# Mamba-2 scan and SiLU block on one core: last outputs transposed by TensorE, a piece of work moved behind unit 1's y, and paced weight loads

## The chip, the cores and the metric

The kernel runs on one core of a Trainium2 chip. The metric is the device time of one execution in microseconds (us). The kernel before the change takes 355.02 us, the median of 7 runs (354.64 to 357.64).

## The reference, cut to what matters

A Mamba-2 scan in chunks gives y for 4 batches, 8 heads, 768 positions and 32 values per head. The heads are laid side by side, which makes 3072 tokens of 256 values. A two-layer block with SiLU follows:

```python
M = CB * L                                   # C.B within a chunk, times decays
y[:, :, sl] = einsum(M, xc) + einsum(Cc, state) * exp(cum)
state = decay_full * state + sum(Bx)
x = y.transpose(0, 2, 1, 3).reshape(3072, 256)
h = x @ w_in                                 # 256 -> 2048
out = (h * (1 / (1 + exp(-h)))) @ w_out      # 2048 -> 256
```

The weights come in 64 bits per value and are turned into 32-bit floats on the chip.

## The kernel before, in words

**Units.** The tokens are cut into 12 units of 256. For each unit the scan makes y, and ScalarE copies it into the tile XM (`f_X`, L469). The first layer of a unit is 8 slots, `f_s1(g, j)` (L479). A slot is 8 matmuls of 128x256 and one SiLU, which writes two of the 16 blocks of the unit's gT. The second layer is a generator for a pair of units (`s2_pair`, L554), and `f_s2(n)` (L621) puts its next n matmuls into the program. From unit 4 on the layers use a scheme with seven instead of eight block products (`f_x1`; `segs` at L558 has the seven products of the second layer, named 1, w, 5, 7, 6, 4, 3).

**Order.** The order is written out by hand, and every engine works in program order. Lines 778 to 847 are the beginning. Unit 0's slots 0, 1 and 2 stand between the steps of unit 1's scan. Then come unit 1's y (`f_Y(1)`, L827), its copy (`f_X(1)`, L828), and the list `steps` (L833), whose entries are unit, slot and work for other engines: `b5` is `w_bits(5)`, `s6` is `w_size(6)`, and `E`, `D`, `T`, `C`, `G`, `Y` are steps of unit 2's scan. The loop at L855 holds unit 2's slots with the second layer of units 0 and 1, and unit 3's y in its last turn.

**Weights.** There are 16 pieces of 512 KB in 64 bits: 0 to 7 are w_in, 8 to 15 are w_out. `load_w(n)` (L150) has SP, the sync engine's queue, load one into one of 7 raw buffers. `w_size(n)` (L160) is two ScalarE instructions, L164 and L166. `w_bits(n)` (L168) is three VectorE instructions, L174, L176 and L178, and an addition on GpSimd, L182. It also posts the load of piece n + 7. Slot j of a unit needs piece j of w_in.

**Loads at the start.** SP posts pieces 0 to 2, then unit 1's B, C and x, then pieces 3 to 6 one after another (L206). Behind them in the same queue come pieces 7 and 8 and the loads of unit 2.

**Outputs.** Products have the model's 256 columns on the partitions and the tokens along them. `f_out` (L542) transposes a tile of 128x256 on VectorE, in blocks of 32x32 (L547), and posts four stores of 32 KB (L549), in which every run is 32 values, 128 bytes. The tile ot of the transposed values has two buffers. For the very last product, "3" of units 10 and 11, the work is split in halves of 128 tokens (L586 to L590). Each half has an addition on VectorE that reads the matmuls' result, a transposition on VectorE, and four stores of 16 KB, of which two go by SP and two by the queue of ScalarE:

```python
for k in range(2):
    nc.vector.tensor_tensor(out=pn[:, :, k], in0=on[:, :, k], in1=..., op=ALU.add)
    f_out(P, 0, 1, p["3"], (nc.sync, nc.scalar), (128 * k, 128 * k + 128))
```

Stores and loads by SP and ScalarE share eight completion semaphores in turn. A DMA instruction first waits until the DMA that last had its semaphore has landed.

Of the kernel before, what the change touches and what calls it, by code (L numbers as in the profile page):

```python
# [8 lines left out]
FP32 = mybir.dt.float32  # L9
# [12 lines left out]
def kernel(  # L22
# [56 lines left out]
    def at(u):  # L79
        return u // UPB, u % UPB * UT  # L80
# [37 lines left out]
    def load_x(u, q):  # L118
        b, t0 = at(u)
        xt[u] = loads.tile([128, 2, H, D], FP32, name="xt")  # L120
        for k in range(2):
            q.dma_start(out=xt[u][:, k], in_=x[b, :, t0 + 128 * k:t0 + 128 * k + 128].rearrange("h p d -> p h d"))
# [27 lines left out]
    def load_w(n, q):  # L150
        src, dst = w_piece(n)
        if src.dtype == FP32:
            q.dma_start(out=dst, in_=src)
            return
        t = raw[n] = rawp.tile([128, 2, WF, 2], U32, name="raw")
        q.dma_start(out=t.rearrange("p k f two -> p k (f two)"), in_=src.bitcast(U32))
# [11 lines left out]
    def w_bits(n, parts=1):  # L168
        dst = w_piece(n)[1]
        if n in raw:  # L170
            u, v, hi = wu.pop(n), wv.pop(n).bitcast(U32), raw[n][:, :, :, 1]


            nc.vector.tensor_scalar(out=u, in0=u, scalar1=LEAST, scalar2=MOST, op0=ALU.max, op1=ALU.min)  # L174
            u = u.bitcast(U32)
            nc.vector.tensor_scalar(out=u, in0=u, scalar1=3, scalar2=None, op0=ALU.logical_shift_left)  # L176

            nc.vector.scalar_tensor_tensor(out=v, in0=hi, scalar=0x80000000, in1=v,  # L178
                                           op0=ALU.bitwise_and, op1=ALU.bitwise_or)
            for i in range(parts):  # L180
                fs = slice(WF // parts * i, WF // parts * (i + 1))
                nc.gpsimd.tensor_tensor(out=dst[:, :, fs].bitcast(U32), in0=u[:, :, fs], in1=v[:, :, fs], op=ALU.add)  # L182
        if n + RAW < len(W):
            load_w(n + RAW, nc.sync)
# [18 lines left out]
    load_n(1, 0, nc.sync)  # L203
    load_n(1, 1, nc.sync)
    load_x(1, nc.sync)
    for n in range(3, RAW):  # L206
        load_w(n, nc.sync)


# [269 lines left out]
    def f_s1(g, j):  # L479
        if j == 0:  # L480
            GTS[g] = new_g()
        xm = XM[g].rearrange("p (w c) t -> p w (c t)", w=2)
        hp = ps_h.tile([128, 2, UT], FP32, name="hp")
        for i in range(2):
            f = 2 * j + i
            for kc in range(KC):
                nc.tensor.matmul(out=hp[:, i], lhsT=w_in_sb[:, kc, f * 128:(f + 1) * 128],  # L487
                                 rhs=xm[:, kc], start=(kc == 0), stop=(kc == KC - 1))
        nc.scalar.activation(GTS[g][:, :, j], hp, AF.Silu)  # L489
        if j == 7:  # L490
            XM.pop(g)
# [47 lines left out]
    def p_add(o, p, q, engine, op=ALU.add):  # L539
        engine.tensor_tensor(out=o, in0=p, in1=q, op=op)  # L540

    def f_out(P, i, v, c, queues=None, cols=None):  # L542

        b, t0 = at(2 * P + v)
        c0, c1 = cols or (0, UT)
        t = opool.tile([128, UT], FP32, name="ot")
        nc.vector.transpose(out=t[:, c0:c1], in_=c[:, c0:c1])  # L547
        for q in range(4):
            (queues or (nc.sync,))[q % len(queues or (0,))].dma_start(  # L549
                out=bass.AP(tensor=out.tensor, offset=out.offset + (b * S + t0 + c0) * d_model + 128 * i + 32 * q,  # L550
                            ap=[[d_model, 32], [32 * d_model, (c1 - c0) // 32], [1, 32]]),
                in_=t[32 * q:32 * q + 32, c0:c1].rearrange("p (b d) -> p b d", d=32))

    def s2_pair(P, final=False, joint=False):  # L554

        adder = nc.vector if final else nc.gpsimd
        p = {}
        segs = (("1", lambda j: wjo[:, 0, 0, j], lambda: gb(P, 0, 0)), ("w", lambda j: wjo[:, 1, 0, j], lambda: gb(P, 1, 0)),  # L558
                ("5", lambda j: SO[0][j // 4][:, j % 4], lambda: TN[P]),
                ("7", lambda j: SO[2][j // 4][:, j % 4], lambda: gb(P, 0, 1)),  # L560
                ("6", lambda j: SO[1][j // 4][:, j % 4], lambda: gb(P, 0, 0)),
                ("4", lambda j: wjo[:, 1, 1, j], lambda: gb(P, 1, 0)),
                ("3", lambda j: SO[3][j // 4][:, j % 4], lambda: gb(P, 1, 1)))

        def end(m, o):

            p[m] = ppool.tile([128, UT], FP32, name="ps")
            on = o.rearrange("p (c k t) -> p c k t", c=2, k=2)
            pn = p[m].rearrange("p (k c t) -> p c k t", c=2, k=2)
            if not (final and m == "3"):  # L570
                nc.scalar.activation(pn, on, AF.Copy)  # L571
            if m == "w":
                p_add(p["w"], p["w"], p["1"], adder)
                PEND.append(partial(f_out, P, 0, 0, p["w"]))
            elif m == "6":
                p_add(p["6"], p["6"], p["1"], adder)
                p_add(p["7"], p["7"], p["6"], adder)
                p_add(p["6"], p["5"], p["6"], adder, ALU.subtract)
                p_add(p["5"], p["5"], p["7"], adder, ALU.subtract)
                PEND.append(partial(f_out, P, 1, 1, p["5"]))  # L580
            elif m == "4":
                p_add(p["4"], p["4"], p["7"], adder)
                PEND.append(partial(f_out, P, 1, 0, p["4"]))
            elif m == "3" and final:

                for k in range(2):  # L586
                    nc.vector.tensor_tensor(out=pn[:, :, k], in0=on[:, :, k],
                                            in1=p["6"].rearrange("p (k c t) -> p c k t", c=2, k=2)[:, :, k],
                                            op=ALU.add)
                    f_out(P, 0, 1, p["3"], (nc.sync, nc.scalar), (128 * k, 128 * k + 128))  # L590
            elif m == "3":
                p_add(p["3"], p["3"], p["6"], adder)
                PEND.append(partial(f_out, P, 0, 1, p["3"]))

        last = NF // 2 - 1
        if joint:
            o = ps_o.tile([128, 2, UT], FP32, name="o_ps")
            for j in range(NF // 2):
                for n, (m, w, g) in enumerate(segs[:2]):
                    nc.tensor.matmul(out=o[:, n], lhsT=w(j), rhs=g()[:, j], start=(j == 0 and n == 0), stop=(j == last),  # L600
                                     skip_group_check=True)
                    if j == last and n == 1:
                        end("1", o[:, 0])
                        end("w", o[:, 1])
                    yield
        for n, (m, w, g) in enumerate(segs):
            if joint and n < 2:
                continue
            if final and n % 2 == 0:
                o = ps_h.tile([128, 2, UT], FP32, name="hp")[:, 0]  # L610
            else:
                o = ps_o.tile([128, 2, UT], FP32, name="o_ps")[:, 0]
            for j in range(NF // 2):
                nc.tensor.matmul(out=o, lhsT=w(j), rhs=g()[:, j], start=(j == 0), stop=(j == last))  # L614
                if j == last:
                    end(m, o)
                yield
# [3 lines left out]
    def f_s2(n):  # L621
        for _ in range(n):
            if S2 and next(S2[0], S2) is S2:
                S2.pop(0)
                f_s2(1)
# [197 lines left out]
    for k in range(2):  # L823
        f_M(1, k)
    f_s1(0, 2)
    w_bits(3)
    f_Y(1)  # L827
    f_X(1)  # L828
    w_size(4)
    w_size(5)  # L830
    w_bits(4)

    steps = ((1, 0, "b5 s6"), (1, 1, "b6 s7"), (0, 3, "b7 s8"), (1, 2, "b8"), (1, 3, "E D"), (0, 4, ""),  # L833
             (1, 4, ""), (0, 5, "T C s9"), (1, 5, "b9 s10"), (0, 6, "G"), (1, 6, "b10 s11"),
             (0, 7, "Y b11 s12"), (1, 7, "b12 s13"))

# [18 lines left out]
    for j in range(8):  # L855
        waiting, PEND[:] = PEND[:], []
        f_s1(2, j)
        if j == 7:
            scan_piece(3, 0, "Y")
        f_s2(2 if j < 2 else 4)  # L860
        if j < len(late):
            w_steps(late[j])
        if j == 2:
            scan_piece(3, 0, "T")
            for q in range(4):
                f_T1(0, q)
        if j == 3:
            f_SO(0)
        scan_piece(3, j, ("", "", "", "E", "DC", "", "G", ""))
        if j in (5, 6):  # L870
            f_SO((2, 1)[j - 5])
        outputs(waiting)
        if j in (2, 5):
            load_unit(4 + j // 3)

        for h in range(2):
            if j in (3, 5, 7):
                f_TS(0, {3: 3, 5: 2, 7: 4}[j], h)
# [88 lines left out]
```

## Time and profile before

| | |
|---|---|
| median of 7 runs | 355.02 us |
| the profiled execution | 354.92 us |
| its span (first to last instruction) | 353.2 us, so 1.72 us lie around it |
| TensorE matmuls (PE) | busy 342.0 us, 97% of the span |
| TensorE weight loads (PEld) | 287.0 us, 81% |
| VectorE (DVE) | 206.1 us, 58% |
| ScalarE (ACT) | 162.0 us, 46% |
| GpSimd (POOL) | 112.0 us, 32% |
| granted TensorE clock, mean | 0.999 |

Times in the timeline count from the start of the span. A row is start, duration, engine, line, operation, output <- input, shape and how often; brackets at its end hold the idle time before it and what ended it. An engine's name with a "q" is its instruction queue, in which DMAs are issued: the row's duration is that of the issue, not of the transfer. The table of waits gives engine, line, what was waited for, total us, times, and the longest.

### The profile page before, as it was taken

The numbers are of one execution on the slowest core, as the hardware profiler recorded it, in microseconds if no ns is written. First come the engines' busy times: TensorE is split into PE (matmuls) and PEld (weight loads), VectorE is DVE, ScalarE is ACT, GpSimd is POOL, SyncE is SP. The second block draws the span as 40 slices with busy tenths as digits, with TensorE's granted clock in tenths as the row PEclk, the third lists the DMA queues.
The fourth block names the chain that finished last, engine by engine and source line by source line (L and its number), as shares of the span: only waits on it lengthen the run. The fifth ranks groups of instructions, "written<-read, shape, count | busy, mean of one in ns | idle before, by whom it ended". The sixth has DMA issues, their size and how long they took to land.

```text
span 353.2 us, 8346 instructions
## 1 busy us (share of the span) xinstructions
PE 342.0 (97%) x3305; PEld 287.0 (81%) x3306; DVE 206.1 (58%) x409; ACT 162.0 (46%) x393; POOL 112.0 (32%) x137
## 2 busy tenths in 40 slices
PE   7979999999999999999999999999999999999993
PEld 3558888878888878888888888888888888888882
DVE  7979999966695754544663553664562322144722
ACT  2558675323313545354645454645445454453110
POOL 4434345353095041244041244041244112052100
PEclk9999999999999999999999999999999999999999
DMA  6998958899786799865189865166504337431203
GB/s 111 223 341 143 328 173 134 164 178 198 131 121 111 118 174 178 152 123 83 20 159 179 157 114 92 16 113 121 100 2 74 67 61 141 75 62 26 36 0 45
DMA packets 118236, 42.79 MB, mean 121 GB/s; under 512 B 103604, under 2 KB 110004, under 8 KB 118196
## 3 DMA queue, kind: packets, MB, share of 16 engines
q1 hardware_dynamic: 110756, 25.67, 36.3%
q0 software_dynamic: 4464, 16.25, 24.7%
q10 hardware_dynamic: 2976, 0.33, 0.7%
q8 instruction: 26, 0.43, 0.5%
q14 instruction: 14, 0.11, 0.1%
HBM read 22.83 MB, written 3.15 MB: 74 GB/s over the span
## 4 chain that ended last, share of the span: by engine, by line
PE 91%; DVE 4%; DMA 2%; issue 1%; ACT 0%; POOL 0%; SPq 0%; ACTq 0%; DVEq 0%
PE o_ps L614 35%; PE hp L669 28%; PE hp L487 15%; PE hp L614 3%; PE gy L463 3%; PE o_ps L600 2%; PE gy L454 2%; PE gy L400 2%; DVE E L299 1%; PE gy L385 1%; DVE wv L178 1%; DMA tbc<-in_C_dram 1%; DMA tbc<-in_B_dram 1%; DMA out_dram<-ot 0%; DVE gT L275 0%
## 5 line engine op out<-in xcount | busy, mean ns | idle before, releaser
L672 DVE TENSOR_TENSOR gT<-hp,p 128x256 f32<-128x256 f32 x64 | 26.9, 420 | 73.7 <-ACT p L683 37.8
L487 PE MATMUL hp<-XM,w_in_sb 128*128 128x256 f32 x256 | 59.7, 382 | 1.9 <-POOL w_in_sb L182 1.2
L614 PE MATMUL o_ps<-gT,w_out_sb 128*128 128x256 f32 x240 | 60.4, 379 | 0.0
L675 ACT ACTIVATE gT<-gT 128x256 f32<-128x256 f32 x96 | 39.7, 414 | 44.0 <-DVE gT L672 44.0
L487 PEld LDWEIGHTS hp<-XM,w_in_sb 128*128 128x128 f32 x256 | 47.9, 190 | 10.0 <-POOL w_in_sb L182 2.3
L540 POOL TENSOR_TENSOR ps<-ps 128x256 f32<-128x256 f32 x35 | 29.4, 839 | 73.8 <-ACT ps L571 72.5
L669 PE MATMUL hp<-raw 128*128 128x256 f32 x192 | 52.7, 380 | 0.0
L614 PEld LDWEIGHTS o_ps<-gT,w_out_sb 128*128 128x128 f32 x240 | 45.4, 190 | 6.3
L535 POOL DMA_DIRECT2D gT<-gT x31 | 27.1, 911 | 68.1 <-DVE TN L526 21.5
L669 PEld LDWEIGHTS hp<-raw 128*128 128x128 f32 x192 | 36.2, 190 | 5.4 <-POOL ps L540 0.6
L683 ACT ACTIVATE p<-hp 128x256 f32<-128x256 f32 x64 | 24.6, 384 | 27.4 <-PE hp L669 25.9
L672 DVE TENSOR_TENSOR gT<-hp,u 128x256 f32<-128x256 f32 x32 | 13.6, 424 | 39.3 <-PE hp L669 39.3
L669 PE MATMUL hp<-XM,w_in_sb 128*128 128x256 f32 x128 | 34.1, 389 | 0.0
L489 ACT ACTIVATE gT<-hp 128x512 f32<-128x512 f32 x32 | 19.0, 595 | 30.2 <-PE hp L487 30.2
L669 PEld LDWEIGHTS hp<-XM,w_in_sb 128*128 128x128 f32 x128 | 23.3, 190 | 4.3 <-issue 1.0
L299 DVE TENSOR_TENSOR_SCAN E<-ab,diag 128x256 f32<-128x256 f32 (+1 forms) x32 | 25.6, 841 | 0.4
L571 ACT ACTIVATE ps<-o_ps 128x256 f32<-128x256 f32 x38 | 14.5, 383 | 23.9 <-PE o_ps L614 21.0
L336 POOL TENSOR_TENSOR BT<-bn,E 128x256 f32<-128x256 f32 x12 | 9.6, 799 | 46.2 <-DVE E L299 40.9
L614 PE MATMUL o_ps<-gT,wv 128*128 128x256 f32 x88 | 22.2, 380 | 0.0
L614 PE MATMUL o_ps<-gT,wu 128*128 128x256 f32 x88 | 22.2, 380 | 0.0
L614 PE MATMUL o_ps<-gT,raw 128*128 128x256 f32 x80 | 20.6, 382 | 0.0
L669 PE MATMUL hp<-raw,w_in_sb 128*128 128x256 f32 x64 | 19.1, 380 | 0.0
(121 smaller groups left out, 518.2 us busy)
## 6 DMA issues: line engine op xcount, KB each, us to landing
gT<-gT POOLq DMA_DIRECT2D x31, 512.0 KB, 6.1
ab<-in_a_dram SPq DMA_DIRECT2D x40, 128.0 KB
raw<-in_moe_w_in_dram SPq DMA_DIRECT2D x8, 512.0 KB
raw<-in_moe_w_out_dram SPq DMA_DIRECT2D x8, 512.0 KB
xt<-in_x_dram SPq DMA_DIRECT2D x24, 128.0 KB
out_dram<-ot SPq DMA_DIRECT2D x92, 32.0 KB
bn<-in_B_dram SPq DMA_DIRECT2D x22, 64.0 KB
tbc<-in_C_dram SPq DMA_DIRECT2D x40, 32.0 KB
```

What stands on the lines that cost most here:

```text
L299: nc.vector.tensor_tensor_scan(out=E[u].rearrange("p k h t -> p (k h t)")[:, Q * g0:Q * (g0 + n)], data0=t.rearrange("p g t -> p (g t)"), ...
L463: nc.tensor.matmul(out=y[32 * q:32 * q + 32, 2 * w + c, 64 * k:64 * k + 64], lhsT=xc[64 * c:64 * c + 64, k, h], rhs=m[64 * c:64 * c + 64, ...
L487: nc.tensor.matmul(out=hp[:, i], lhsT=w_in_sb[:, kc, f * 128:(f + 1) * 128], rhs=xm[:, kc], start=(kc == 0), stop=(kc == KC - 1))
L489: nc.scalar.activation(GTS[g][:, :, j], hp, AF.Silu)
L535: nc.gpsimd.dma_start(out=o[:, js], in_=a[:, js], accum_op=ALU.add)
L540: engine.tensor_tensor(out=o, in0=p, in1=q, op=op)
L571: nc.scalar.activation(pn, on, AF.Copy)
L614: nc.tensor.matmul(out=o, lhsT=w(j), rhs=g()[:, j], start=(j == 0), stop=(j == last))
L669: nc.tensor.matmul(out=o, lhsT=w, rhs=x_, start=start, stop=True, skip_group_check=True)
L672: nc.vector.tensor_tensor(out=o, in0=p, in1=q, op=ALU.add)
L675: nc.scalar.activation(o, i, AF.Silu)
L683: nc.scalar.activation(o, i, AF.Copy)
```

## The change

1. **Paced loads.** Before pieces 5 and 6 are posted, SP posts a copy of 4 bytes out of piece 3's (then piece 4's) raw buffer into a new tile `mark`. It can be issued only when that piece has landed.
2. **Slot (0, 3)**, unit 0's fourth, moves from the third place of `steps` to just behind `f_Y(1)` and `f_X(1)`. `w_size(4)` and `w_bits(4)` move ahead of `f_Y(1)`; `E D` stays with the fifth entry of `steps`, and slot (0, 3) now stands ahead of the list.
3. **Second layer of units 0 and 1.** In the turns of the loop at L855 with four matmuls of it, these are asked for as two and two. In the last turn unit 3's y (`scan_piece(3, 0, "Y")`) now stands between them; before, it stood ahead of all four.
4. **The last product.** Each half is transposed by TensorE (a matmul against the identity into an hp buffer), copied to ot by ScalarE (first half) or VectorE (second half), and stored by one DMA of 64 KB whose runs are 512 bytes: the first half by SP, the second by ScalarE's queue.

```diff
+    mark = const.tile([1, RAW], U32, name="mark")
     for n in range(3, RAW):
+        if n > 4:
+            nc.sync.dma_start(out=mark[:, n:n + 1], in_=raw[n - 2][0:1, 0, 0, 0:1])
         load_w(n, nc.sync)
...
-                    f_out(P, 0, 1, p["3"], (nc.sync, nc.scalar), (128 * k, 128 * k + 128))
+                    tp = ps_h.tile([128, 512], FP32, name="hp")[:, 0:128]
+                    nc.tensor.transpose(out=tp, in_=p["3"][:, 128 * k:128 * k + 128], identity=ident)
+                    ot = opool.tile([128, UT], FP32, name="ot")[:, 0:128]
+                    if k == 0:
+                        nc.scalar.activation(ot, tp, AF.Copy)
+                    else:
+                        nc.vector.tensor_copy(out=ot, in_=tp)
+                    b, t0 = at(2 * P + 1)
+                    r = b * S + t0 + 128 * k
+                    (nc.sync, nc.scalar)[k].dma_start(out=out[r:r + 128, 0:128], in_=ot)
...
     f_s1(0, 2)
+    w_size(4)
     w_bits(3)
+    w_bits(4)
     f_Y(1)
     f_X(1)
-    w_size(4)
     w_size(5)
-    w_bits(4)
-
-    steps = ((1, 0, "b5 s6"), (1, 1, "b6 s7"), (0, 3, "b7 s8"), (1, 2, "b8"), (1, 3, "E D"), (0, 4, ""),
+    f_s1(0, 3)
+
+    steps = ((1, 0, "b5 s6"), (1, 1, "b6 s7"), (1, 2, "b7 s8"), (1, 3, "b8"), (0, 4, "E D"),
...
         f_s1(2, j)
+        f_s2(2)
         if j == 7:
             scan_piece(3, 0, "Y")
-        f_s2(2 if j < 2 else 4)
+        if j > 1:
+            f_s2(2)
```

`f_out` also loses its options for queues and columns, which nothing else used.

More of the change, by code (lines that the diff above doesn't have):

```diff
@@ L540, in p_add, with f_out @@
         engine.tensor_tensor(out=o, in0=p, in1=q, op=op)
-    def f_out(P, i, v, c, queues=None, cols=None):
+    def f_out(P, i, v, c):
         b, t0 = at(2 * P + v)
-        c0, c1 = cols or (0, UT)
         t = opool.tile([128, UT], FP32, name="ot")
-        nc.vector.transpose(out=t[:, c0:c1], in_=c[:, c0:c1])
+        nc.vector.transpose(out=t, in_=c)
         for q in range(4):
[L549 to L552, printed above, removed]
+            nc.sync.dma_start(
+                out=bass.AP(tensor=out.tensor, offset=out.offset + (b * S + t0) * d_model + 128 * i + 32 * q,
+                            ap=[[d_model, 32], [32 * d_model, UT // 32], [1, 32]]),
+                in_=t[32 * q:32 * q + 32].rearrange("p (b d) -> p b d", d=32))
     def s2_pair(P, final=False, joint=False):
```

## The prediction

> **What bounds the kernel now.** I read the page first, then the waits of PE, then the timeline of the three places where the waits or the end point. The page gives PE 97% of the span and the chain that ended last 91% PE, so only two things shorten it: time in which PE is idle, and time after its last matmul. The table of waits, asked for PE alone from 26 us to 348 us, has two lines:
>
> ```profile
> PE gy L454 <- ACT gT L489: 0.7, 1, 0.7
> PE hp L487 <- ACT XM L472: 0.7, 1, 0.7
> ```
>
> In these 322 us the table by stages gives PE 320.5 us busy, and the two lines are 1.4 us of the rest. Whatever other engines do there is covered. The first of the two in time is unit 1's copy of y:
>
> ```profile
> 24.51 1.24 PE L463 MATMUL gy<-E,xt 64*32 64x64 f32 x64
> 24.78 1.27 POOL L182 TENSOR_TENSOR w_in_sb<-wu,wv 128x512 uint32<-128x512 uint32 x1 [2.87 <-DVE wv L178]
> 25.79 0.60 ACT L472 ACTIVATE XM<-gy 128x512 f32<-128x512 f32 x1 [1.20 <-PE gy L463]
> 26.44 14.08 PE L487 MATMUL hp<-XM,w_in_sb 128*128 128x256 f32 x64 [0.69 <-ACT XM L472]
> ```
>
> PE ends unit 1's y at 25.75, ScalarE copies it until 26.39, and the next slot, (1, 0), can start at 26.44. Piece 3 of the weights (the POOL row) is ready at 26.05. The second is unit 3's y:
>
> ```profile
> 75.76 1.99 PE L487 MATMUL hp<-XM,w_in_sb 128*128 128x256 f32 x8
> ...
> 77.03 1.28 DVE L411 TENSOR_TENSOR E<-gy,E 128x512 f32<-128x512 f32 x2
> ...
> 78.45 0.58 PE L454 MATMUL gy<-cw,sm 32*64 32x64 f32 x24 [0.70 <-ACT gT L489]
> ```
>
> The bracket names ScalarE, but the row that ends just before is VectorE's L411, at 78.31; PE had ended its slot at 77.75. Third, the end, from the timeline, the chain and SP's waits. The last matmul ends at 347.62:
>
> ```profile
> 347.66 0.29 DVE L587 TENSOR_TENSOR ps<-hp,ps 128x128 f32<-128x128 f32 x1 [2.08 <-PE hp L614]
> 347.99 0.31 DVE L547 STREAM_TRANSPOSE ot<-ps 128x128 f32<-128x128 f32 x1
> 348.25 0.29 DVE L587 TENSOR_TENSOR ps<-hp,ps 128x128 f32<-128x128 f32 x1
> ...
> 348.73 0.31 DVE L547 STREAM_TRANSPOSE ot<-ps 128x128 f32<-128x128 f32 x1 [0.18 <-DMA out_dram<-ot]
> ```
> ```profile
> 350.64 0.32 SPq L549 DMA_DIRECT2D out_dram<-ot  x1
> ```
> ```profile
> 346.95 1.65 DMA out_dram<-ot
> ```
> ```profile
> SPq L549 <- DMA out_dram<-ot: 1.0, 1, 1.0
> ```
>
> All values of the second half are in SBUF at 349.04, yet the last store is issued at 350.64, because it waited 1.0 us for an earlier store (the last fence, from SP's waits). Eight stores by two queues are in the way, not the transposition. A store takes 1.65 us from issue to landing (the chain's row), so the last lands near 350.64 + 1.65 = 352.29, and the closing barrier takes 0.91 us to 353.2.
>
> **Slot (0, 3) behind unit 1's y.** After unit 1's y PE no longer needs the copy but piece 3, at 26.05; PE began 0.06 us after such a row at 21.90. That is 26.11. If VectorE works beside it (bits 4 now follows at once), the addition takes 1.39 as at 28.71 instead of 1.27, and PE starts at 26.23. Gain 26.44 - 26.11 = 0.33, or 0.21; I take 0.27. What hides the copy now is slot (0, 3), 1.73 us. On ScalarE `w_size(4)` stands ahead of the copy: from the end of a SiLU at 24.59 its two instructions (26.28 to 27.50, 1.22) last until 25.81, so the copy starts at 25.81 instead of 25.79; far from late, since PE wants it at 27.85. If piece 4 had not landed at 24.6, the copy would be late by as much (see the loads below). Slots 3 and on are one slot later in ScalarE's order, so `w_size(6)` starts near 30.2 instead of 29.05, but VectorE's work on pieces 4 and 5 is 1 to 2 us earlier; no slot comes to wait for its piece (slot (0, 5), which needs piece 5, runs at 38.5, piece 5 is converted at 32.5 even now).
>
> **Two matmuls ahead of unit 3's y.** Two matmuls of 0.43 us (8 take 1.73 in the chain) fill 77.75 to 78.61, and L411 has ended at 78.31. Their data are there: the accumulating DMA into gT was issued by POOL from 64.24 on, such DMAs land after 5.4 to 8.0 us, and the buffer o_ps was copied out at 75.24. So the whole 0.70 goes. What is late next: unit 3's slots need its copy. y ends near 79.98, the copy near 80.65, and PE has two matmuls, 0.86 plus about 0.2 of restart (1.92 instead of 1.73 in the row after y), until 81.0. A margin of 0.3; if it were gone, each 0.1 costs 0.1. Gain 0.70 to 0.40; I take 0.65.
>
> **Paced loads.** Two semaphore waits and two small DMAs more on SP. Behind them in SP's queue stand pieces 5 to 8, all loads of unit 2, and pieces 9 on. Between 18 us and 27 us the DMA moves 348 GB/s: 0.524 MB per piece is 1.51 us, and pieces 3 to 8 are just these 9 us. So piece 3 is complete near 19.5 and piece 4 near 21.0. Piece 5 is now posted near 20.9 (19.5 + landing + two issues of 0.45) where it was posted before 18.5; bytes of a store show up 0.8 us after its issue. So the line runs dry 0.5 to 0.8 us per mark, and all that follows comes 1 to 1.5 us later. Nothing before PE was waiting for a load in this stretch, so nothing is gained by it. Piece 5 (near 23.5) is read at 26.5; of unit 2, the decays are issued by 31.8 and read at 39.87; piece 9 is issued at 34.87 and read at 42.05, 7.2 us later, while a piece takes at most 6.0 us from its posting behind others (16.49) to ScalarE's reading it (22.49). Slack 1.2 us at the least there. Cost 0; bounds 0 and the rival below.
>
> **The last product.** Removed: two transpositions and eight stores. Added, per half: a weight load of 0.14 and a matmul of 0.27 (L351, same shape, 0.48 from the start of the load to the end), a copy from PSUM, one store. First half: addition ends 347.95, PE starts 0.11 later (as L454 after L411), ends 348.54; ScalarE starts 0.09 later; its copy lies between 0.28 (128 columns on the line through 0.384 for 256 and 0.595 for 512) and 0.39 (L434, 128x128); I take 0.30: 348.93, store issued, landed near 350.6. Second half: its addition follows at once, to 348.25; PE ends near 348.75; VectorE's copy is between 0.19 (L424, 64 columns) and 0.29 (L587); its buffer ot is free when product 4's stores have landed, 348.60, as before; done at 349.05. That is no earlier than the 349.04 of before. But its store is issued at 349.1 instead of 350.64, and it has no predecessor to wait for: 350.64 - 349.1 = 1.54 less. The one unknown is how long a store of 64 KB takes. No row shows one; 32 KB took 1.65. Below: as the last one of 16 KB, about 1.4 to SP's wait, gain 1.8. Above: the two halves one after the other, 1.65 each from 348.93, lands 352.2, gain 0.1. Loads show that bytes are cheap here (64 KB at 348 GB/s is 0.19 us), so I stay near the 32 KB row and add 0.2: gain 1.35.
>
> [...]
>
> **Sum.** 0.27 + 0.65 + 0 + 1.35 = 2.27. From the profiled execution, 354.92 - 2.27 = 352.65; it stands 0.1 below the median of 355.02. I predict 352.6. PE is gap-free between the places, so what is gained early is carried to the end: the triggers of all later transfers move with PE.
>
> **Rivals.**
> - *The store of 64 KB is slow, or the two halves queue.* For it: no row has this form, and both use the same engines. Against: the two copies are 0.1 apart and small. The end gains only 0.1 to 0.8, say 0.4: 354.92 - 0.92 - 0.4 = 353.6. Chance 0.17.
> - *A wait takes the place of the one removed:* piece 3 later than 26.4, or unit 3's copy after the two matmuls. For: margins of 0.3. Against: rows of two engines give the margin. Gains 0.2 instead of 0.92: 354.92 - 0.2 - 1.35 = 353.4. Chance 0.1.
> - *Slower: the marks hold SP's queue.* An SP issue behind a full queue took 3.3 to 3.5 us (tbc at 10.49 and 22.32). If both marks met this, everything behind comes 6.8 us later; with the least slack of 1.2 to some 4 us, ScalarE stalls at piece 9 (42 us), SiLUs wait behind it and PE loses 2.8 to 5.6, say 4.2: 354.92 - 2.27 + 4.2 = 356.8. It decides when the delay passes about 2.3 plus the slack, 3.5 to 6.3 us. Against: the marks come when the queue holds just one piece. Chance 0.05.
> - The edits do what they say; the order of instructions on each engine leaves no doubt.
>
> **How the numbers follow.** The forecast has 0.68, own range 352.0 to 353.1 (gains 0.21 + 0.4 + 1.1 at the least, 0.33 + 0.70 + 1.8 at the most). With the two lesser gains the range is 351.9 to 353.8; it leaves out the slower case and the ends. Faster or slower by over 0.5%, 1.78 us, about what a measurement of this kernel can tell, means below 353.24 or above 356.8. Forecast nearly whole, and a third of the lesser gains, lie below: faster 0.76; same 0.20; slower 0.04.
>
> **What would show it.** Right: PE's waits from 26 us on have no L454 line, and at L487 at most 0.4; unit 3's y (L454) directly behind two matmuls of L614's group; last store issued 1.4 to 1.6 us after the last matmul (now 3.0); the end 4.1 to 4.3 after it (now 5.6). Wrong: a wait of ScalarE for a raw piece, PE idle between 30 and 50 us, or a store that takes over 2 us.

## The result and the profile after

The changed kernel takes 353.4 us (median of 18 runs, 352.69 to 354.68) against 355.12 us for the kernel before (47 runs, 354.25 to 357.64). The ratio is 0.9947, 95% interval [0.9935, 0.9958]: faster by 0.53%, with 0.42% to 0.65% as its bounds, so about at the 0.5% that the prediction set as measurable (the two medians alone are 0.48% apart). The forecast was 352.6, its range 351.9 to 353.8. The forecast's own part of that range, 352.0 to 353.1, does not hold the result; the wider range, which takes in the rivals' lesser gains, does. The profiled execution took 353.18 us, with a span of 351.5 us.

In the changed kernel the lines of the code have moved: f_s1's matmuls are L491 (were L487), the two parts of y L458 and L467 (L454, L463), the mark is L210, the transpositions of the last product are L595, their copies L598 and L600, their stores L603.

The table of PE's waits of the changed kernel, from 26 us on (engine, line, what was waited for, total us, times, longest):

```profile
PE hp L491 <- POOL w_in_sb L182: 0.7, 1, 0.7
PE hp L595 <- DVE ps L590: 0.4, 1, 0.4
```

The line of unit 3's y is gone, and the wait for the copy XM is now one for piece 3 on GpSimd (POOL). The second line is the new transposition, behind the last matmul. The timeline of the changed kernel at the first place:

```profile
24.68 0.86 PE L467 MATMUL gy<-E,xt 64*32 64x64 f32 x64
24.94 1.28 POOL L182 TENSOR_TENSOR w_in_sb<-wu,wv 128x512 uint32<-128x512 uint32 x1 [2.87 <-DVE wv L178]
...
25.79 0.59 ACT L476 ACTIVATE XM<-gy 128x512 f32<-128x512 f32 x1
...
26.27 1.99 PE L491 MATMUL hp<-XM,w_in_sb 128*128 128x256 f32 x8 [0.74 <-POOL w_in_sb L182]
```

Slot (0, 3) starts 0.05 us after piece 3 is ready (24.94 + 1.28 = 26.22), no longer behind ScalarE's copy, which ends at 26.38. Executions begin up to 1.2 us apart (the first slot starts anywhere between 15.03 and 16.24 us in the profiles of this study), so distances from the first slot say more than times: from the first slot to this one it is 10.82 us, and it was 11.16. The second place:

```profile
75.59 1.99 PE L491 MATMUL hp<-XM,w_in_sb 128*128 128x256 f32 x8
...
76.86 1.28 DVE L415 TENSOR_TENSOR E<-gy,E 128x512 f32<-128x512 f32 x2
...
77.42 1.03 PE L627 MATMUL o_ps<-gT,wu 128*128 128x256 f32 x4
...
78.38 0.58 PE L458 MATMUL gy<-cw,sm 32*64 32x64 f32 x24
```

The second layer's matmuls (L627) fill the time until VectorE's L415 ends at 78.14, and y follows them without a gap. (The row counts four: each of the two matmuls that `f_s2(2)` asks for is two instructions in the trace, as the four of `f_s2(4)` were eight in the kernel before.) From the slot behind unit 1's y to the last matmul it is 320.42 us, and it was 321.18. Third, the end. The last matmul ends at 346.69:

```profile
346.73 0.49 DVE L590 TENSOR_TENSOR ps<-hp,ps 128x128 f32<-128x128 f32 x2 [2.08 <-PE hp L627]
347.07 0.59 PE L595 MATMUL hp<-ident,ps 128*128 128x128 f32 x2 [0.38 <-DVE ps L590]
347.44 0.28 ACT L598 ACTIVATE ot<-hp 128x128 f32<-128x128 f32 x1 [3.73 <-PE hp L595]
347.74 0.36 SPq L603 DMA_DIRECT2D out_dram<-ot  x1
348.15 0.29 DVE L600 COPY ot<-hp 128x128 f32<-128x128 f32 x1 [0.94 <-PE hp L595]
348.47 0.37 ACTq L603 DMA_DIRECT2D out_dram<-ot  x1
```

The last store is issued 1.79 us after the last matmul (it was 3.02), and the span ends 4.79 after it (it was 5.58). VectorE's copy of the second half starts at 348.15, though TensorE had transposed that half by 347.66.

The sum of the traces: -0.34 (first place) - 0.76 (second place, with 0.06 of restarts) - 0.79 (end) + 0.17 (this execution's first slot came at 15.45 instead of 15.28) = -1.72, which is the difference of the spans, 353.20 - 351.48.

### The profile page after: what moved, and what is told of

The parts are those of the page before. It is cut to its first block, busy times and chain, and to the rows that moved or that the text cites. A ratio compares the mean times of both kernels' runs of the same rounds, so it can differ in the third digit from the quotient of the medians.

```text
span 351.5 us, 8348 instructions
## 1 busy us (share of the span) xinstructions
PE 342.4 (97%) x3307; PEld 287.2 (82%) x3308; DVE 205.5 (58%) x408; ACT 162.5 (46%) x394; POOL 111.1 (32%) x137
## 4 chain that ended last, share of the span: by engine, by line
PE 90%; DVE 5%; DMA 2%; issue 1%; POOL 0%; SPq 0%; ACTq 0%; ACT 0%; DVEq 0%
PE o_ps L627 36%; PE hp L682 28%; PE hp L491 14%; PE hp L627 3%; PE gy L467 2%; PE o_ps L613 2%; PE gy L404 2%; PE gy L458 2%; DVE E L303 1%; PE gy L389 1%; DVE wv L178 1%; DVE E L415 1%; DMA tbc<-in_C_dram 1%; DMA tbc<-in_B_dram 1%; DVE st L430 0%
## 5 line engine op out<-in xcount | busy, mean ns | idle before, releaser
L491 PE MATMUL hp<-XM,w_in_sb 128*128 128x256 f32 x256 | 59.6, 382 | 2.0 <-POOL w_in_sb L182 2.0
L627 PE MATMUL o_ps<-gT,w_out_sb 128*128 128x256 f32 x240 | 60.4, 379 | 0.0
L491 PEld LDWEIGHTS hp<-XM,w_in_sb 128*128 128x128 f32 x256 | 47.9, 190 | 10.0 <-POOL w_in_sb L182 3.3
L627 PEld LDWEIGHTS o_ps<-gT,w_out_sb 128*128 128x128 f32 x240 | 45.4, 190 | 6.3
L627 PE MATMUL o_ps<-gT,wu 128*128 128x256 f32 x88 | 22.4, 380 | 0.0
L627 PE MATMUL o_ps<-gT,wv 128*128 128x256 f32 x88 | 22.2, 380 | 0.0
L627 PE MATMUL o_ps<-gT,raw 128*128 128x256 f32 x80 | 20.6, 382 | 0.0
```

## The experiments

The theory to test: the parts add up; the end gains because two stores take the place of eight, and part of that gain is lost to the buffers ot; the marks cost nothing because the loads behind them have slack. The rivals: the transposition by TensorE is itself what gains; a store of 64 KB is slow; the marks carry the gain, or take some of it away.

**Each part alone.** The last product alone (e1), on the kernel before:

```diff
-                    f_out(P, 0, 1, p["3"], (nc.sync, nc.scalar), (128 * k, 128 * k + 128))
+                    tp = ps_h.tile([128, 512], FP32, name="hp")[:, 0:128]
+                    nc.tensor.transpose(out=tp, in_=p["3"][:, 128 * k:128 * k + 128], identity=ident)
...
+                    (nc.sync, nc.scalar)[k].dma_start(out=out[r:r + 128, 0:128], in_=ot)
```

> The kernel before with the last product's part alone. Theory (the four parts add up, each worth what its place in the two traces shows): the span falls from 353.2 to about 352.4, since the end after the last matmul takes 4.8 us in place of 5.6; the last matmul itself ends near 347.6. Rival (the end gained nothing by itself, the change came from the earlier parts): span 353.0 to 353.4 and 5.4 us or more after the last matmul. By the prediction's own sizes: 4.2 us after it, span 351.9.

Measured: 354.63 us (353.97 to 357.25) beside 355.48 of the kernel before, ratio 0.9974 [0.9955, 0.9994]. The profile has 4.93 us behind the last matmul, 0.65 less than before. The end is not the same in every execution: the four profiles with the old end (before, e2, e3, e7) have 5.58, 5.72, 5.44 and 5.30 us, and the three with the new one (changed, e1, e4) 4.79, 4.93 and 4.95. So the 0.79 above is that of one pair, and the means differ by 0.62. The profiled execution is itself longer than the median, with a span of 355.5 us, for a reason told under the hardware below.

The two matmuls ahead of unit 3's y alone (e2):

```diff
+        f_s2(2)
         if j == 7:
             scan_piece(3, 0, "Y")
-        f_s2(2 if j < 2 else 4)
+        if j > 1:
+            f_s2(2)
```

> The kernel before with the two matmuls of the second layer ahead of unit 3's y, nothing else. Theory: PE's wait at L454 near 78 us (0.70) is gone and nothing takes its place, so the last matmul ends at 346.9 to 347.0 and the span is 352.5. Rival (a wait takes the place of the one removed): the last matmul stays at 347.4 or later.

Measured: 354.58 us (353.9 to 355.36), ratio 0.9961 [0.9942, 0.9981]. PE's waits from 26 us on keep one line of the two:

```profile
PE hp L487 <- ACT XM L472: 0.7, 1, 0.7
```

From the slot behind unit 1's y to the last matmul it is 320.42 us, the same as in the changed kernel. The whole gain of the second place is this part.

Slot (0, 3) alone (e3), with `w_size(4)` and `w_bits(4)` moved and no marks:

```diff
+    w_size(4)
     w_bits(3)
+    w_bits(4)
     f_Y(1)
...
+    f_s1(0, 3)
-    steps = ((1, 0, "b5 s6"), (1, 1, "b6 s7"), (0, 3, "b7 s8"), (1, 2, "b8"), (1, 3, "E D"), (0, 4, ""),
+    steps = ((1, 0, "b5 s6"), (1, 1, "b6 s7"), (1, 2, "b7 s8"), (1, 3, "b8"), (0, 4, "E D"),
```

> The kernel before with slot (0, 3) moved behind unit 1's y, with the conversion of piece 4 ahead of y, and without the paced loads. Theory: the slot starts when piece 3 is ready, 0.2 to 0.35 us earlier than slot (1, 0) did relative to unit 1's y; span 352.9. Rival (piece 4 or 5 has not landed without the pacing, and ScalarE stops at it): a wait of ScalarE for a raw piece near 25 us, the copy of y late, span 353.3 or more.

Measured: 355.02 us (354.45 to 356.05), ratio 0.9979 [0.9959, 0.9999]. From the first slot to this one it is 10.84 us, 0.32 less than before, and PE waits 0.55 us there for piece 3. The profiled execution began late (first slot at 16.24), so its span says nothing.

The changed kernel without the two marks (e4):

```diff
-        if n > 4:
-            nc.sync.dma_start(out=mark[:, n:n + 1], in_=raw[n - 2][0:1, 0, 0, 0:1])
```

> The changed kernel without the two small copies that pace the loads. Theory (the marks only make what stands behind them on SP later, 3 to 4 us, and the slack just covers it): the span stays at 351.3 to 351.6, ScalarE's wait of 1.1 us for piece 9 near 43 us is gone, and piece 9 is posted near 35 instead of 39 us. Rival (the marks are needed for piece 4 at 24.6 us): ScalarE waits for it, PE waits at slot (1, 0) or behind, the span grows by 0.3 or more.

Measured: 353.36 us (352.63 to 353.83), ratio 0.9932 [0.9914, 0.9951]. In these four runs on one chip the three parts alone gave 0.85 + 0.90 + 0.46 = 2.21 us, and together 2.12. As far as intervals of some 0.7 us to either side can tell, they add. From the first slot to slot (0, 3) it is 10.83 us without the marks and 10.82 with them, so at this place they change nothing.

**The marks alone** (e7), on the kernel before:

```diff
+    mark = const.tile([1, RAW], U32, name="mark")
     for n in range(3, RAW):
+        if n > 4:
+            nc.sync.dma_start(out=mark[:, n:n + 1], in_=raw[n - 2][0:1, 0, 0, 0:1])
```

> The kernel before with the paced loads alone. Theory A (pacing gains nothing and costs nothing, since the loads behind it have slack): slot (1, 0) starts 0.3 to 0.7 us after unit 1's y as before, time within 0.2 us of before; ScalarE waits about 1 us for piece 9. Theory B (the stop without a named cause in the middle of unit 1's y, 0.29 us in the profile of before and 1.62 us in that of the last product's part alone, is program text that arrives late behind the weight pieces): there is no such stop at L463, and slot (1, 0) starts 0.3 us earlier, and the median is 0.2 to 0.6 us lower.

Measured: 354.94 us (353.96 to 356.54) beside 354.89, ratio 0.9989 [0.9968, 1.0011]. PE's waits from 26 us on are the two of the kernel before, and a third:

```profile
...
PE o_ps L355 <- DMA bn<-in_B_dram: 0.6, 1, 0.6
```

The slot behind unit 1's y starts 0.39 us earlier than in the kernel before (10.77 us after the first slot), because unit 1's y ran without a stop (0.86 instead of 1.24 us, see the hardware below). PE then gives 0.61 us back at 40.77, waiting for unit 2's B, and 0.93 by the last matmul (322.11 from that slot, where it was 321.18). These sizes come from this one profile; the medians show no balance that can be measured.

This run also bounds what moving slot (0, 3) is worth. Where y runs without a stop, the slot behind it starts at 10.77 without the move, no later than the 10.82 of the changed kernel. The move keeps the start at 10.82 to 10.84 where y has a stop of up to 0.55 us (e3, e4, e6). So its 0.34 us is the gain over an execution with a stop of that size.

**Four stores or one?** (e6) The changed kernel, with TensorE's transposition kept and each half stored in four parts, as before the change:

```diff
-                    (nc.sync, nc.scalar)[k].dma_start(out=out[r:r + 128, 0:128], in_=ot)
+                    for q in range(4):
+                        (nc.sync, nc.scalar)[q % 2].dma_start(out=out[r:r + 128, 32 * q:32 * q + 32],
+                                                              in_=ot[:, 32 * q:32 * q + 32])
```

> The changed kernel with its halves transposed by TensorE, but each half stored by four stores of 128 rows x 32 columns, by SP and ScalarE's queue in turn, as before the change. Theory (the gain of the end is that of having two stores and not eight): the last store is issued 3 us or more after the last matmul, the end comes 5.5 us or more after it, as before. Rival (the gain is that of the transposition on TensorE): the end stays near 4.8 us.

Measured: 354.39 us (354.01 to 355.01), ratio 0.9975 [0.9958, 0.9992]. The end is 6.41 us, longer than the 5.58 of the kernel before. Of SP's waits behind 345 us the longest, and SP's row of the stores:

```profile
SPq L604 <- DMA out_dram<-ot: 1.6, 1, 1.6
```
```profile
347.42 3.26 SPq L604 DMA_DIRECT2D out_dram<-ot  x4
```

With eight stores the wait of one store for another is back, 1.6 us (it was 1.0), and SP's last of four is issued 3.98 us after the last matmul. So TensorE's transposition with as many stores as before loses 6.41 - 5.58 = 0.83 us, and the number of stores gains 6.41 - 4.79 = 1.62. Each size is that of one pair of profiles, and the 0.83 isn't the transposition alone: VectorE's copy comes 0.49 us late here too (see e5). The medians agree: 354.89 - 354.39 = 0.50 is less than the two other places gain, 0.34 + 0.76. In the changed kernel the first half takes 0.99 us from the start of its addition to the end of its copy (346.73 to 347.72), and before it took 0.64 to the end of its transposition (347.66 to 348.30). So the path by TensorE, with ScalarE's copy behind it, was the slower one here, by 0.35 us.

**Buffers of their own for the two halves** (e5). The changed kernel, with the halves copied into two idle tiles of another pool instead of the two buffers ot:

```diff
-                    ot = opool.tile([128, UT], FP32, name="ot")[:, 0:128]
+                    ot = sc.tile([128, UT], FP32, name=("p1", "p5")[k])[:, 0:128]
```

> The changed kernel, but the two transposed halves go into buffers that are idle at the end (p1 and p5), in place of ot's two, so that VectorE's copy of the second half no longer waits for product 4's stores. Theory (the copy, which starts 0.49 us after TensorE's second transposition, is held by those stores): it starts 0.05 us after the transposition, the last store is issued near 1.35 us after the last matmul in place of 1.78, and the end comes 4.4 us after it in place of 4.8. Rival (something else holds the copy, such as SP's issue of the first half's store, at whose end it starts): the copy stays 0.4 to 0.5 us behind the transposition and the end stays at 4.8 us.

Measured: 352.11 us (351.94 to 352.39) beside 354.89, ratio 0.9902 [0.9873, 0.9931]. With e9 below it is the fastest kernel of this study. Its rows of the end, after a last matmul that ends at 346.78:

```profile
347.17 0.59 PE L595 MATMUL hp<-ident,ps 128*128 128x128 f32 x2 [0.39 <-DVE ps L590]
...
347.79 0.29 DVE L600 COPY p<-hp 128x128 f32<-128x128 f32 x1 [0.48 <-PE hp L595]
...
348.12 0.37 ACTq L603 DMA_DIRECT2D out_dram<-p  x1
```

VectorE's copy follows the transposition (ends 347.75) by 0.05 us, where it came 0.49 later in the changed kernel. The last store is issued 1.33 us after the last matmul instead of 1.79, and the span ends 2.55 after that instead of 3.00. The first 0.46 is the wait on ot. The second 0.45 comes with it, and SP's closing wait for the stores (L977) falls from 1.8 to 1.1 us. The DMA packets of the traces suggest where most of it lies. Counted from the last matmul, in the changed kernel a packet of 8 KB on the queue that the profile calls instruction runs from 2.12 to 2.76 us (much the same in e1 and e4). The last eight packets of the first store start at 2.76. Fifteen of the sixteen packets of 4 bytes that come with the last store's 128 of 512 bytes are done by 3.01, the last comes at 3.35. With buffers of their own both stores are complete at 2.57, and that packet starts at 2.50 (2.49 to 2.64 in e8 to e10). That it holds up one DMA engine is argued from these times; no run moved it.

The same without marks (e8, the diff of e4 and that of e5 together):

> The changed kernel with own buffers for the two halves and without the paced loads. If the copy is held by product 4's stores and the marks are worth nothing: 0.4 us less than the changed kernel, span 351.1. If the marks keep program text from arriving late: a stop of 0.2 to 1.6 us at unit 1's y and a span 0.2 or more above that of the kernel with own buffers and marks.

Measured: 352.62 us (352.46 to 352.99), ratio 0.9917 [0.9885, 0.9948]. The end is 4.02 us (3.89 with marks), and unit 1's y had a stop of 0.71 us. Its six runs all lie above the six of e5 on the same chip (351.94 to 352.39), so here the marks went with a gain of 0.5 us, where alone (e7) they gained nothing. Of the 0.41 us between the two profiles, 0.43 lies ahead of the first slot (15.53 and 15.10), before a mark is issued (20.95). What the marks are worth is not settled.

**How much pacing does the kernel bear?** First one mark alone (e9, ahead of piece 5), then three (e10), each of which waits for the piece just before it; both with buffers of their own:

```diff
-        if n > 4:
+        if n == 5:
```
```diff
-        if n > 4:
-            nc.sync.dma_start(out=mark[:, n:n + 1], in_=raw[n - 2][0:1, 0, 0, 0:1])
+        if n > 3:
+            nc.sync.dma_start(out=mark[:, n:n + 1], in_=raw[n - 1][0:1, 0, 0, 0:1])
```

> The changed kernel with its own buffers for the two halves at the end, and only the first of the two marks (ahead of piece 5). Two marks gave 352.11 us and piece 9 posted near 39 us, no mark 352.62 and 35 us. Theory (each mark holds SP until one piece has landed, and delays all that follows by 1.5 to 2 us): piece 9 posted between 36.5 and 37.5 us, ScalarE waits for no raw piece, PE loses nothing, 352.1 to 352.6 us. Rival (the delay is set by how full the line of transfers is and not by the number of marks): piece 9 posted within 0.5 us of 39 or of 35. The stop of PE in the middle of unit 1's y: if it comes from program text fetched behind weight pieces, it is at most 0.3 us, since piece 5 is held until the fetch has passed; if it is independent of the loads, it varies from run to run as before, 0.2 to 1.6.

> The changed kernel with its own buffers at the end, and a mark ahead of each of pieces 4, 5 and 6 that waits for the piece just before it: one piece under way at a time. This puts a price on stronger pacing. Theory (the loads' slack of about 4 us is what hides the marks, and two marks use it up): everything behind comes 2 to 4 us later again, piece 9 is posted at 41 to 43 us, ScalarE waits 2 to 5 us for it, SiLUs are late, and PE loses 0.5 to 3 us between 26 and 50 us: 352.6 to 355 us. Rival (there is still slack behind ScalarE): ScalarE waits longer but PE has no gap, and the time is that with two marks, 352.1 us within 0.4.

Measured: one mark, 352.21 us (351.81 to 352.27), ratio 0.9906 [0.9892, 0.9919]; three marks, 356.93 us (355.22 to 359.17), ratio 1.005 [1.0027, 1.0073], slower than the kernel before. The waits of PE in the one with three marks, from 26 us on:

```profile
PE o_ps L355 <- DMA bn<-in_B_dram: 1.9, 1, 1.9
...
PE hp L491 <- ACT gT L493: 0.4, 1, 0.4
```

The load of unit 2's B, bn, and piece 9 stand in SP's queue behind the marks. When each was issued, and what it cost:

| kernel | marks | bn issued, us | piece 9 issued, us | ScalarE waits for piece 9 | PE waits for bn |
|---|---|---|---|---|---|
| before | 0 | 31.83 | 34.87 | 0 | 0 |
| own buffers, one mark | 1 | 33.20 | 36.18 | 0.3 | 0 |
| changed kernel | 2 | 35.04 | 39.05 | 1.1 | 0 |
| four stores | 2 | 35.05 | 39.21 | 2.1 | 0 |
| own buffers | 2 | 35.99 | 39.79 | 2.5 | 0.4 (its weight load) |
| marks alone | 2 | 36.45 | 40.31 | 1.8 | 0.6 |
| own buffers, three marks | 3 | 38.99 | 42.74 | 2.0 | 1.9 |

The table of PE's waits has no line for bn in the kernel with own buffers and two marks, but PE's weight load for L355 waited 0.4 us for it, and the row is longer than the 0.38 us that it takes in the changed kernel:

```profile
40.04 0.59 PE L355 MATMUL o_ps<-ident,bn 128*128 128x128 f32 x2
```

From slot (0, 3) to the last matmul it takes 320.86 us, 0.44 more than the changed kernel. So PE loses nothing when bn is issued by 35.05 us, and loses time at 35.99 and later. The same two marks put bn at 35.04 to 36.45 in four profiles: the changed kernel stands less than 1 us short of a loss, and executions differ by more than that. One mark was expected to post piece 9 between 36.5 and 37.5 with no wait of ScalarE; it came at 36.18, 0.3 earlier, and ScalarE waited 0.3. With three marks PE's own waits are 2.3 us, and from slot (0, 3) to the last matmul it is 323.47 us, 3.05 more than in the changed kernel. The profiled execution was the fastest of its eight.

## Why the prediction was right, step by step

- **Slot (0, 3).** Predicted 0.27 (0.21 to 0.33), measured 0.34, and 0.32 alone. The bound was named rightly: PE starts 0.05 us behind piece 3. The wait there was to be at most 0.4 and is 0.74. That costs nothing: unit 1's y ran 0.38 shorter, and PE stood waiting for the same piece 3 that much longer. The prediction took the length of y for given; without the stop in it the move gains nothing (e7).
- **Two matmuls ahead of unit 3's y.** Predicted 0.65 (0.40 to 0.70), measured 0.70 and 0.06 of restarts. What was late next, unit 3's copy, made no gap: the trace has no idle PE between 26.27 us and the last matmul.
- **Paced loads.** "Cost 0" held, but its working failed at the step "So the line runs dry 0.5 to 0.8 us per mark, and all that follows comes 1 to 1.5 us later". SP's queue in the changed kernel:

```profile
16.29 1.42 SPq L156 DMA_DIRECT2D raw<-in_moe_w_in_dram  x2
21.16 0.69 SPq L210 DMA_DIRECT2D mark<-raw  x1
21.89 0.38 SPq L156 DMA_DIRECT2D raw<-in_moe_w_in_dram  x1
22.39 0.60 SPq L210 DMA_DIRECT2D mark<-raw  x1
...
25.26 4.12 SPq L107 DMA_DIRECT2D tbc<-in_C_dram  x2
29.42 5.58 SPq L95 DMA_DIRECT2D ab<-in_a_dram  x4
35.04 1.25 SPq L107 DMA_DIRECT2D bn<-in_B_dram  x2
```

Piece 3 had landed by 21.16, not 19.5. The 348 GB/s were a mean from 18 to 27 us. The changed kernel's rate in 40 slices of 0.2 us from 16 to 24 us shows why they can't be used from 18 on:

```profile
GB/s 122 120 116 113 140 106 159 200 214 184 165 67 47 72 72 266 420 379 420 369 399 410 399 420 399 399 338 246 72 20 0 0 0 0 41 164 133 317 246 246
```

The first 15 slices, to 19.0 us, have 126 GB/s on the mean. (Of their 2810 packets from 16 to 19 us 2774 are under 512 bytes, so these are nearly all packets of other loads.) The zeros from 22.0 to 22.8 are the line run dry, 0.8 us for both marks together, where 0.5 to 0.8 was told for each. What follows came 3.2 us (bn) and 4.2 us (piece 9) later instead of 1 to 1.5: the issues at L107 and L95 took as long as before (4.12 and 5.58 us, before 4.26 and 5.92), so most of the delay in SP's queue was passed on: 3.7 us at the first L107, 3.6 at L95, 3.2 at bn. The slack was larger too: piece 9, given 1.2 us, made ScalarE wait 1.05 us after coming 4.2 later, so it had about 3.1; and PE lost nothing by ScalarE's wait. The two errors cancelled, and that is luck: the delay was two to four times what was told.
- **The last product.** This is the term that was mis-sized: 1.35 predicted (0.1 to 1.8), 0.79 measured, and that is most of the difference between the forecast and the result. Its terms: the last store issued 1.48 us after the last matmul, measured 1.79; from there to the end of the span 2.56 + 0.2, measured 3.00. The failed step is "its buffer ot is free when product 4's stores have landed, 348.60, as before; done at 349.05". The landing came as told, 0.97 us after the last matmul, but the copy began 0.49 later. The chain of the changed kernel:

```profile
346.02 1.64 DMA out_dram<-ot
...
347.69 0.05 DVEq L600
347.74 0.41 issue
348.15 0.29 DVE ot L600
```

The chain goes through product 4's store, and after VectorE's queue has seen it (DVEq), 0.41 us pass in which the profile shows nothing. Without the shared buffer they are gone (e5), and the end is 5.58 - 3.89 = 1.69 us shorter than before, near the upper end of 1.8. A reused buffer was counted as free once its store had landed; here it cost 0.46 us more than that on the way to the last store.
- **The rivals.** The 64 KB store isn't slow by its size: with buffers of its own the last one takes 2.55 to 2.69 us from its issue to the end, as the 16 KB ones do (2.43 to 2.56). With the shared pair it takes 3.00 to 3.16 (changed, e1, e4). So the forecast's first rival came near by its price (353.6, gain of the end 0.1 to 0.8; the result is 353.4 and 0.79), and part of its effect was there, but not by its cause. The slower case exists: three marks cost 356.93 - 352.21 = 4.7 us beside one on the same chip, and it was priced at 4.2. (The profile, of the fastest execution, shows 323.47 - 320.62 = 2.85 of it behind slot (0, 3).) It decides about where the prediction put it, when the delay of bn passes some 4 us (4.2 in e5, 4.6 in e7), but at another place: PE waits for bn at L355, before ScalarE's wait for piece 9 reaches PE.
- **The sum.** 2.27 predicted; the profiled executions differ by 354.92 - 353.18 = 1.74. The end is 0.56 short, the slot 0.07 and the matmuls 0.11 over, and this execution began 0.17 later. The step from there to the forecast has a sign wrong: the profiled execution stands 0.1 below the median, so 352.65 belongs to a median of 352.75, and the forecast's own range to 352.2 to 353.3. The result is above that too.
- **The signs.** Of the prediction's signs of being right two came: no L454 line, and y directly behind the two matmuls. Three did not: the wait at the slot is 0.74 and not at most 0.4, the last store is issued at 1.79 and not at 1.4 to 1.6, the end takes 4.79 and not 4.1 to 4.3. One of its signs of being wrong came, a wait of ScalarE for a raw piece (1.1 us); it cost PE nothing.

## What to carry to other kernels

At the end of a kernel count the stores and the buffers first: a slower transposition (by 0.35 us for the first half) that allows one store instead of four gained 0.79 us in one pair of profiles (0.62 between the means), and two idle tiles instead of a recycled pair nearly 0.9 more. A wait put into a load queue can delay what stands behind it by far more than the time the transfers stand still: two marks let the line run dry for 0.8 us and made bn 3.2 to 4.6 us late. It need not be passed on whole: the one mark of e9 kept SP from its next piece from 17.50 to 21.59 us, and bn came 1.4 us late. So list the first reader of each load behind it, and how long before its use the load is issued. A small gain of one place is best measured between two events of the same trace, since here executions began up to 1.2 us apart.

## What the runs showed of the hardware

**A stop of PE that nothing in the profile releases.** In unit 1's y (L463 or L467) PE stops after the first four instructions of the row. The timeline of the kernel with the last product alone:

```profile
24.43 0.30 PE L463 MATMUL gy<-E,xt 64*32 64x64 f32 x4
26.35 0.81 PE L463 MATMUL gy<-E,xt 64*32 64x64 f32 x60 [1.62 <-issue]
```

The stop is 1.62 us here, 0.71 in e8, 0.25 in e2, and 0.2 to 0.4 in the kernel before, e3 and e4 (by the length of the row, 1.05 to 1.24 instead of 0.86): in all six profiles without marks. With marks it is in one of six (e6, 0.55). Each of the seven stops ends 1.2 to 1.5 us after the end of a packet of 16 KB on the queue that the profile calls instruction. In the five profiles without a stop that packet had ended by 23.20 us, 1.3 us or more before y's row starts. The expectations of e7, e8 and e9 weighed that the stop is a wait for program text that comes late. Of such text the profiles show only this queue (26 packets and 0.43 MB in the kernel before) and these times. If the stop is a wait for such a packet, it held PE in seven of twelve profiles. That it is one is argued from the times alone, and why the packet is late stays open. In six of the seven the packet ran while the DMA moved 323 to 400 GB/s. In e6, with marks, the DMA moved 31 GB/s from 22.78 to 23.76 us while the packet ran, and the stop was there all the same. So loads beside it are not the whole cause, and that the marks let the packet pass is not shown.

**The clock after a stop.** In the same execution the slots behind the stop ran slower. The table by stages of the kernel with the last product alone (window, length, busy us by engine, granted TensorE clock, DMA share, GB/s):

```profile
26.00:45.00 19.00, 17.96 (x134) 15.52 (x134) 15.75 (x21) 11.87 (x22) 6.69 (x5) 0.91 0.96 249
```

The granted clock is 0.91 here; in the changed kernel without marks it is 1.00 in the same window. PE had been idle for 1.62 + 0.69 = 2.31 of 3.1 us. From there to the last matmul it took 322.76 us, 1.58 more than the kernel before, so the stop and what followed it cost 1.62 + 1.58 = 3.2 us in that execution. The trace has the granted clock at 0.50 from 27.64 to 31.05, which is 3.41 us, and at 1.00 ahead of it and behind it. Half the clock for 3.41 us loses 1.7 us, which is 9% of 19 us and fits the 0.91; it is also about the 1.58. In the 3.41 us ahead of the slow stretch PE was busy for 1.32 us. That this idle time set the clock back is the author's reading of one execution; no run varied that time.
